# First attention scores of block 1 placed behind the first input products, a dearer instruction fetch in the list, and B22 staged in other buffers

## The chip, the cores and the metric

The kernel runs on one core of a Trainium2 chip. The core has five engines with an instruction queue each: TensorE (PE in the profile, its weight loads PEld), VectorE (DVE), ScalarE (ACT), GpSimd (POOL, idle here) and SyncE (SP, which only starts DMA transfers). An engine works through its queue in order; engines wait for each other by semaphores. The metric is the device time of one execution in microseconds (us), lower is better.

## The reference

Attention with a narrow window, then two feed-forward layers, on 2304 tokens of width 512:

```python
scores = q @ k.T / sqrt(64); heads 0-3: 0 <= rel < 32; heads 4-7: 0 <= rel < 128 and rel % 4 == 0
x = softmax(scores) @ v                    # 4 x 8 heads x 576 tokens x 64, laid out as (2304, 512)
h = x @ w_in;  P = a0 + a1 h + a2 h^2 + a3 h^3;  Q = 1 + |b0||h| + |b1| h^2
x = (P / (Q + 1e-6)) @ w_out               # layer 1, 512 -> 2048 -> 512
h = x @ w_in2; x = (max(h,0) + alpha min(h,0)) @ w_out2   # layer 2
```

## The kernel before

**Tiling.** Attention is cut into 18 units of 256 tokens and four heads each (a plain and a dilated one per token range). Layer 1 works on five token blocks (256, then four of 512 columns), with tokens along the free axis. For each block, 16 chunks ("items") of 128 hidden features are made by `inproj` (L608 to L619: products into one of two PSUM banks `ps_h`), go through the rational function on ScalarE and VectorE (`rat_1`, `rat_2`, the last step of the first block writing the tile `gl` at L650), and return through `outproj1` (L661, L669) into the four banks `ps_y`. Block 0 runs in plain fp32 (one product per weight tile, seen as two matmul records); the later blocks are split into a high and a low fp32r part with three products each. Layer 2 works on blocks of 384 tokens, two at a time, by a Strassen-like scheme: seven products `product` (L828) per pair of chunks, on operands named B11, T2, B21, T3, T4, T1 and B22 (`st_pair`, from L846).

**Attention of a unit.** `att_s` makes scores (a mask by bf16 matmuls, L468, then 32 fp32 products, L478) into two banks; `att_max`, `att_exp`, `att_den`, `att_norm`, `att_t` make the transposed probabilities `pts`; `att_pv` (L551) multiplies by the values; `att_hi`/`att_lo` copy the result into the layer's input `xh`, `xl`. Units 0 and 1 make block 0's input. Unit 2 is the first of block 1. Its scores stand in the loop at L984, ahead of block 0's input products.

**What sets the order.** The program is written as nested loops, and then `in_order_of_need` (L155) lists the instructions of each engine anew, up to 197 us of its own clock, by longest path to the end. It holds a cost per instruction (`_cost`, L111) and counts a delay on TensorE each time 256 instructions have been passed (`FETCH`, `FETCH_NS`, `FETCH_END`, L38 to L40 and L275). After that point the framework's scheduler orders the rest.

**The seam between the layers.** `x_load(0)` (L751) reads layer 1's output back from DRAM into staging tiles; B22's two halves were put into the attention buffers `p` and `pts` (L758). `x_combine` makes T1 to T4 from them, `x_place` splits each operand into its two parts (L726 on ScalarE, L727 on VectorE). The first pair's `v1` and `u2` (L863, L858) use the same two buffers `pts` and `p`.

**Weights.** The first weights arrive as 64-bit words and are converted on ScalarE (L392) and VectorE (L395, L397) before they can be multiplied.

Of the kernel before, what the change touches and what calls it, by code (L numbers as in the profile page):

```python
# [37 lines left out]
FETCH = 256  # L38
FETCH_NS = 3800
FETCH_END = 30e3  # L40
QB = 32
# [112 lines left out]

def in_order_of_need(tc, nc, places):  # L155

# [17 lines left out]
    for k, i in enumerate(todo):  # L174
# [36 lines left out]
        for kind, regions in (("r", reads), ("w", writes)):  # L211
            for place, p0, p1, f0, f1 in regions:
                have = seen.setdefault(place, [])
                if kind == "w":
                    have[:] = [x for x in have if not (p0 <= x[2] and x[3] <= p1 and f0 <= x[4] and x[5] <= f1)]
                have.append((k, kind, p0, p1, f0, f1))
    after = [[] for _ in range(n)]
    for k in range(n):
# [75 lines left out]
def attn_rational_prelu_kernel(  # L294
# [158 lines left out]
    def att_s(U, tags=("aS", "aP"), banks=None):  # L453
# [12 lines left out]
        for p in range(2):  # L466
            for j0, j1 in zip(runs[p], (*runs[p][1:], HALF)):
                nc.tensor.matmul(  # L468
                    out=s[p][:, j0 * CELL:j1 * CELL].rearrange("p (t k) -> p t k", k=CELL),
                    lhsT=ident16,  # L470
                    rhs=mask[kinds[p][j0]].unsqueeze(1).to_broadcast([128, j1 - j0, CELL]),
                    start=(j0 == 0), stop=False,
                )
        for jj in range(HALF):
            for i in range(HEADS):
                for p in range(2):
                    at = jj * HEADS + i
                    nc.tensor.matmul(  # L478
                        out=s[p][quad(i), jj * CELL:(jj + 1) * CELL],
                        lhsT=a["q"][rows(p), at * QB:(at + 1) * QB],  # L480
                        rhs=a["k"][rows(p), at * CELL:(at + 1) * CELL],
                        start=False, stop=(jj == HALF - 1),
                    )

    def att_max(U):
# [121 lines left out]
    def inproj(item):  # L607
# [9 lines left out]
        for k, (w, x) in enumerate(pairs):  # L617
            nc.tensor.matmul(out=hp, lhsT=w, rhs=x, start=(k == 0), stop=(k == len(pairs) - 1))  # L618
        h_t[item] = hp  # L619

    def pair_tiles(J):
# [84 lines left out]

    todo = []

    def out_some(k):
# [39 lines left out]
    def x_load(n):  # L749
# [3 lines left out]
        if n == 0:  # L753
# [3 lines left out]
            st["T3"], st["T1"] = t[:, :2 * BLK], t[:, 2 * BLK:]  # L757
            st["B22"] = [ap_.tile([128, BLK], F32, tag=s, name="st_b22") for s in ("p", "pts")]  # L758
            st["T2"] = st["T4"] = rawp.tile([128, 2 * DM], F32, tag="u", name="st_t2", bufs=1)[:, :2 * BLK]
# [224 lines left out]
    for k in range(4):  # L984
        if k < 3:
            att_s(k, sets[(k + 2) % 3])
        if k == 2:
            qk_load(3)
        if 0 <= k - 1 < 2:
            att_den(k - 1)  # L990
            att_norm2(k - 1)
        if k < 3:
            att_max(k)
            att_exp(k)
# [6 lines left out]
        with tc.high_priority(-100):  # L1001
            if k == 1:
                root_b1()
            for _ in range((0, 2, 2, 1)[k]):
                w_next(1)
    att_den(2)
    att_norm(2)
    att_t(2)

    for J in range(NP):  # L1010
        U = 2 + (J + 1) // 2
        new = J % 2 and U < NU
        last = J % 2 and U <= NU
        if last:
            banks = [bank(tag) for tag in ("aS", "aP")]
            att_pv(U - 1, banks)
            if new:
                v_load(U)
                att_s(U, banks=banks)
            if U + 1 < NU:  # L1020
                qk_load(U + 1)
        if new:
            att_max(U)
        if J >= NC and early and (J - NC) * 5 // 9 > (J - NC - 1) * 5 // 9:
            w_early(*early.pop(0))
        pair_tiles(J)
        for item in items[2 * J:2 * J + 2]:
            inproj(item)
        if J < NC // 2:
# [77 lines left out]
    out_some(len(todo))  # L1107
    in_order_of_need(tc, nc, slots)

# [76 lines left out]
```

## Time and profile before

| | |
|---|---|
| median of 3 runs | 875.23 us (874.51 to 875.78) |
| profiled execution | 874.21 us, of which the span of instructions is 872.4 us |
| TensorE busy | 845.8 us, 97% of the span |
| VectorE busy | 721.5 us, 83% |
| ScalarE busy | 559.9 us, 64% |
| mean granted TensorE clock | 0.938 of full speed |

The profile is one execution. The difference between 874.21 and 872.4 lies outside the first and last instruction. "Idle before" names what ended an engine's wait; "issue" means that nothing recorded ended it. The granted clock is given as a share of 2.4 GHz: 0.95 is the higher of its two levels, 0.50 the lower (1.2 GHz).

### The profile page before, as it was taken

How to read it: one execution, taken by the hardware profiler on the slowest of the kernel's cores; microseconds unless marked ns; L12 is line 12 of the kernel's file. 1: busy time of each engine (PE TensorE's matmuls, PEld its weight loads, DVE VectorE, ACT ScalarE, POOL GpSimd, SP SyncE). 2: the span in 40 equal slices, each digit the busy share in tenths (PEclk: the TensorE clock that was granted, in tenths of full speed). 3: DMA queues.
4: the chain of work that ended last, by engine and by line, in shares of the span. 5: the costliest groups of instructions: out<-in, count | busy, mean ns of one | idle time of the engine just before them, and what ended most of it. 6: DMA issues, size and time to landing. Idle time of an engine off the chain costs nothing. (4 is left out here: it accounts for less than half of the span.)

```text
span 872.4 us, 15592 instructions
## 1 busy us (share of the span) xinstructions
PE 845.8 (97%) x6258; PEld 719.1 (82%) x6260; DVE 721.5 (83%) x1066; ACT 559.9 (64%) x1092; POOL 0.2 (0%) x4
## 2 busy tenths in 40 slices
PE   7899999999999999999999899999999999999998
PEld 4677878888888777788888798998989989899896
DVE  4699999988989878899999698898976778767652
ACT  4799987777866786766766366557463546645424
POOL 0000000000000000000000000000000000000000
PEclk8799999999999999999999899999999999999999
DMA  9792211123631344322202233215220102300001
GB/s 351 308 371 97 64 61 49 53 100 122 236 121 56 117 160 173 116 83 94 87 25 97 85 142 100 97 61 154 82 86 24 49 25 79 119 28 25 0 1 73
DMA packets 33912, 90.93 MB, mean 104 GB/s; under 512 B 4016, under 2 KB 11568, under 8 KB 33840
## 3 DMA queue, kind: packets, MB, share of 16 engines
q1 hardware_dynamic: 33840, 89.94, 29.3%
q8 instruction: 49, 0.80, 0.4%
q14 instruction: 23, 0.19, 0.1%
HBM read 74.72 MB, written 15.20 MB: 103 GB/s over the span
## 5 line engine op out<-in xcount | busy, mean ns | idle before, releaser
L618 PE MATMUL ps_h<-xh,winh 128*128 128x512 f32 x256 | 102.1, 399 | 4.2 <-DVE tc L639 4.2
L618 PE MATMUL ps_h<-xl,winh 128*128 128x512 f32 x256 | 100.3, 392 | 0.6 <-DVE xl L588 0.6
L669 PE MATMUL ps_y<-gh,wouth 128*128 128x512 f32 x256 | 99.4, 390 | 0.9 <-ACT gh L658 0.9
L669 PE MATMUL ps_y<-gl,wouth 128*128 128x512 f32 x256 | 100.2, 391 | 0.0
L669 PE MATMUL ps_y<-gh,woutl 128*128 128x512 f32 x256 | 100.0, 391 | 0.0
L618 PE MATMUL ps_h<-xh,winl 128*128 128x512 f32 x256 | 99.8, 390 | 0.0
L636 ACT ACTIVATE ta<-ps_h,root 128x512 f32<-128x512 f32 (+1 forms) x80 | 52.4, 655 | 54.5 <-DVE tc L649 33.8
L689 PE MATMUL ps_y<-woutl,gh 128*128 128x512 f32 x192 | 74.9, 390 | 0.0
L689 PE MATMUL ps_y<-wouth,gl 128*128 128x512 f32 x192 | 74.9, 390 | 0.0
L689 PE MATMUL ps_y<-wouth,gh 128*128 128x512 f32 x192 | 74.8, 389 | 0.0
L726 ACT ACTIVATE st_a<-w 128x1024 fp32r<-128x1024 f32 x24 | 25.3, 1056 | 60.7 <-PE ps_h L828 55.2
L833 ACT ACTIVATE n<-h 128x768 f32<-128x768 f32 x48 | 40.5, 843 | 37.0 <-DVE gl L727 21.0
L618 PEld LDWEIGHTS ps_h<-xh,winh 128*128 128x128 f32 x256 | 48.0, 188 | 17.0 <-DVE tc L639 6.5
L637 ACT ACTIVATE tc<-ps_h,co 128x512 f32<-128x512 f32 (+1 forms) x80 | 59.8, 748 | 0.0
L835 DVE SCALAR_TENSOR_TENSOR n<-n,alp,h 128x768 f32<-128x768 f32 x48 | 48.7, 1016 | 13.0 <-ACT h L834 12.4
L638 DVE TENSOR_TENSOR tc<-tc,ps_h 128x512 f32<-128x512 f32 (+1 forms) x80 | 50.3, 628 | 10.0 <-ACT tc L637 9.8
L669 PEld LDWEIGHTS ps_y<-gh,wouth 128*128 128x128 f32 x256 | 48.1, 188 | 11.6 <-ACT gh L658 1.3
L618 PEld LDWEIGHTS ps_h<-xl,winh 128*128 128x128 f32 x256 | 48.1, 188 | 10.5 <-DVE xl L588 1.0
L669 PEld LDWEIGHTS ps_y<-gh,woutl 128*128 128x128 f32 x256 | 48.3, 189 | 10.0
L618 PEld LDWEIGHTS ps_h<-xh,winl 128*128 128x128 f32 x256 | 48.1, 188 | 10.2
L669 PEld LDWEIGHTS ps_y<-gl,wouth 128*128 128x128 f32 x256 | 48.2, 188 | 9.9
L639 DVE SCALAR_TENSOR_TENSOR tc<-tc,co,ps_h 128x512 f32<-128x512 f32 (+1 forms) x80 | 54.9, 686 | 0.2
(187 smaller groups left out, 2164.3 us busy)
## 6 DMA issues: line engine op xcount, KB each, us to landing
ld_qk<-in_qk_dram SPq DMA_DIRECT2D x16, 768.0 KB, 5.4
w<-w_dram_in SPq DMA_DIRECT2D x24, 512.0 KB, 3.2
raw<-in_w_in_dram SPq DMA_DIRECT2D x16, 512.0 KB, 5.3
raw_inh<-in_w_out_dram SPq DMA_DIRECT2D x13, 512.0 KB, 6.5
out_dram<-os SPq DMA_DIRECT2D x18, 256.0 KB, 2.1
raw_inh<-in_w_in_dram SPq DMA_DIRECT2D x8, 512.0 KB, 8.3
raw_outh<-in_w_in_dram SPq DMA_DIRECT2D x8, 512.0 KB, 9.1
raw_outh<-in_w_out_dram SPq DMA_DIRECT2D x8, 512.0 KB, 9.2
```

The source lines that it names most:

```text
L618: nc.tensor.matmul(out=hp, lhsT=w, rhs=x, start=(k == 0), stop=(k == len(pairs) - 1))
L636: nc.scalar.activation(out=ta, in_=hp, func=AF.Abs, scale=root)
L637: nc.scalar.activation(out=tc_, in_=hp, func=AF.Identity, scale=co[:, 3:4], bias=co[:, 2:3])
L638: nc.vector.tensor_tensor(out=tc_, in0=tc_, in1=hp, op=ALU.mult)
L639: nc.vector.scalar_tensor_tensor(out=tc_, in0=tc_, scalar=co[:, 1:2], in1=hp, op0=ALU.add, op1=ALU.mult)
L669: nc.tensor.matmul(out=yt, lhsT=w[:, m * 128:(m + 1) * 128], rhs=g, start=(c == 0 and i == 0), stop=(c == NC - 1 and i == len(pairs) - 1),)
L689: nc.tensor.matmul(out=yt, lhsT=g[:, tok], rhs=w, start=(first and i == 0), stop=(last and i == 2))
L726: nc.scalar.activation(out=hi, in_=t, func=AF.Copy)
L833: nc.scalar.activation(out=neg, in_=h, func=AF.Relu, scale=-1.0)
L835: nc.vector.scalar_tensor_tensor(out=neg, in0=neg, scalar=alp[:, c:c + 1], in1=h, op0=ALU.mult, op1=ALU.subtract, reverse1=True)
```

## The change

Five edits: (1) the list's fetch delay goes from 3800 to 6500 ns and is counted up to 45 instead of 30 us; (2) unit 2's scores, maximum, exponentials and normalisation move from the lead-in loop into the main loop's first pass (`J == 0`), behind the input products of block 0's items 0 and 1; (3) a list `late` ties the first score product of unit 2 behind the last input product of item 1; (4) the load of unit 3's q and k follows there; (5) B22's staging tiles take the buffers `v` (one) and `os` (one of two, otherwise used for output copies).

```diff
-FETCH_NS = 3800
-FETCH_END = 30e3
+FETCH_NS = 6500
+FETCH_END = 45e3
...
-def in_order_of_need(tc, nc, places):
+def in_order_of_need(tc, nc, places, late):
...
+    at = {i.name: k for k, i in enumerate(todo)}
+    for b, a in late:
+        behind[at[b]].add(at[a])
...
-            st["B22"] = [ap_.tile([128, BLK], F32, tag=s, name="st_b22") for s in ("p", "pts")]
+            st["B22"] = [
+                ldp.tile([128, BLK], F32, tag=s, name="st_b22", bufs=b) for s, b in (("v", 1), ("os", 2))
+            ]
...
-        if k < 3:
+        if k < 2:
             att_s(k, sets[(k + 2) % 3])
-        if k == 2:
-            qk_load(3)
...
-    att_den(2)
-    att_norm(2)
-    att_t(2)
...
-        new = J % 2 and U < NU
+        new = (J % 2 or J == 0) and U < NU
         last = J % 2 and U <= NU
-        if last:
+        if J == 0:
+            pair_tiles(J)
+            inproj(items[0])
+            ahead = inproj(items[1])
+        if new or last:
             banks = [bank(tag) for tag in ("aS", "aP")]
-            att_pv(U - 1, banks)
+            if last:
+                att_pv(U - 1, banks)
             if new:
-                v_load(U)
-                att_s(U, banks=banks)
+                if J:
+                    v_load(U)
+                scores = att_s(U, banks=banks)
+                if J == 0:
+                    late.append((scores, ahead))
```

The edits shift line numbers: L478, L551, L618, L669 of before are L482, L557, L624, L676 now; L636 to L659 are 7 higher, L726 and L727 are L734 and L735, L863 is L873.

**First place: TensorE, behind the attention values of units 0 and 1.** `ps_h_482` (before) and `ps_h_416` (now) are item 0, `ps_h_487` and `ps_h_421` item 1; `ps_aS`, `ps_aP` with `ld_qk_146` are unit 2's scores. Before:

```order
L551 MATMUL ps_y0_243<-p_288,ld_v_136 64x32 x2
L551 MATMUL ps_y1_244<-p_288,ld_v_136 64x32 x2
L618 MATMUL ps_h_482<-xh0_410,win0_308 128x256
L478 MATMUL ps_aS_320<-ld_qk_146 32x64
L478 MATMUL ps_aP_321<-ld_qk_146 32x64
```

Now:

```order
L557 MATMUL ps_y0_243<-p_288,ld_v_136 64x32 x2
L557 MATMUL ps_y1_244<-p_288,ld_v_136 64x32 x2
L624 MATMUL ps_h_416<-xh0_357,win0_308 128x256 x2
L624 MATMUL ps_h_416<-xh1_404,win0_308 128x256 x2
L624 MATMUL ps_h_421<-xh0_357,win0_308 128x256 x2
L624 MATMUL ps_h_421<-xh1_404,win0_308 128x256 x2
L482 MATMUL ps_aS_426<-ld_qk_146 32x64
L482 MATMUL ps_aP_427<-ld_qk_146 32x64
```

Seven of the eight products of items 0 and 1 moved ahead of unit 2's scores.

**Second place: TensorE, ahead of unit 2's values** (`ps_aS` from `pts` and `ld_v_148`). `ps_h_613` and `ps_h_618` are items 2 and 3, `ps_h_690` is item 4. Before:

```order
L618 MATMUL ps_h_613<-xh0_410,win2_314 128x256 x2
L618 MATMUL ps_h_613<-xh1_457,win2_314 128x256 x2
L618 MATMUL ps_h_618<-xh0_410,win2_314 128x256 x2
L618 MATMUL ps_h_618<-xh1_457,win2_314 128x256 x2
L551 MATMUL ps_aS_527<-pts_477,ld_v_148 64x32 x2
```

Now:

```order
L624 MATMUL ps_h_618<-xh0_357,win2_314 128x256 x2
L624 MATMUL ps_h_618<-xh1_404,win2_314 128x256 x2
L676 MATMUL ps_y0_735<-gl_506,wout0_360 128x256
L676 MATMUL ps_y1_736<-gl_506,wout0_360 128x256
L676 MATMUL ps_y2_737<-gl_506,wout0_360 128x256
L676 MATMUL ps_y3_738<-gl_506,wout0_360 128x256
L624 MATMUL ps_h_690<-xh0_357,win4_366 128x256 x2
L624 MATMUL ps_h_690<-xh1_404,win4_366 128x256
L557 MATMUL ps_aS_527<-pts_513,ld_v_148 64x32 x2
```

Four output products (they need `gl_506`, the first pair's result, and `wout0`) and three of item 4 moved ahead of unit 2's values.

**Third place: the seam, ScalarE.** `gh_5171` is the high part of layer 1's last pair, `v1_5189` the copy of the first Strassen product out of its bank `ps_h_5175`. Before:

```order
L726 ACTIVATE st_B22h_5161<-st_b22_4813 128x384
L646 ACTIVATE ta_5086<-tb_5087,c1t_109 128x1024
L726 ACTIVATE st_B22h_5161<-st_b22_4814 128x384
L647 ACTIVATE ta_5086<-ta_5086 128x1024
L658 ACTIVATE gh_5167<-tc_4998 128x1024
L658 ACTIVATE gh_5171<-tc_5088 128x1024
L863 ACTIVATE v1_5189<-ps_h_5175 128x384
```

Now:

```order
L734 ACTIVATE st_B22h_5161<-st_b22_4814 128x384
L653 ACTIVATE ta_5086<-tb_5087,c1t_109 128x1024
L654 ACTIVATE ta_5086<-ta_5086 128x1024
L873 ACTIVATE v1_5189<-ps_h_5175 128x384
L665 ACTIVATE gh_5171<-tc_5088 128x1024
```

`v1` now stands ahead of `gh_5171`, which needs VectorE's `tc_5088`.

The same place on VectorE: `gl_5168` and `gl_5172` are the low parts of layer 1's last two pairs, `st_s_5193`, `st_a_5199` and `st_s_5201` prepare the second Strassen pair. Before:

```order
L649 SCALAR_TENSOR_TENSOR tc_5088<-tc_5088,co_105,ta_5086 128x1024
L727 TENSOR_TENSOR st_B22l_5162<-st_b22_4813,st_B22h_5161 128x384
L650 SCALAR_TENSOR_TENSOR tc_5088<-tb_5087,tc_5088 128x1024
L727 TENSOR_TENSOR st_B22l_5162<-st_b22_4814,st_B22h_5161 128x384
L659 TENSOR_TENSOR gl_5168<-tc_4998,gh_5167 128x1024
L659 TENSOR_TENSOR gl_5172<-tc_5088,gh_5171 128x1024
L858 TENSOR_TENSOR u2_5190<-v1_5189,ps_h_5182 128x384
```

Now:

```order
L656 SCALAR_TENSOR_TENSOR tc_5088<-tc_5088,co_105,ta_5086 128x1024
L666 TENSOR_TENSOR gl_5168<-tc_4998,gh_5167 128x1024
L657 SCALAR_TENSOR_TENSOR tc_5088<-tb_5087,tc_5088 128x1024
L868 TENSOR_TENSOR u2_5190<-v1_5189,ps_h_5182 128x384
L749 TENSOR_TENSOR w32_5084<-w32_5084 128x256
L749 TENSOR_TENSOR st_s_5193<-w32_5084,st_s_5193 128x256
L666 TENSOR_TENSOR gl_5172<-tc_5088,gh_5171 128x1024
L735 TENSOR_TENSOR st_a_5199<-w32_5084,st_a_5198 128x1024
L735 TENSOR_TENSOR st_s_5201<-st_s_5193,st_s_5200 128x768
L421 TENSOR_TENSOR woutl2_5209<-w32_5206,wouth2_5208 128x1024
```

`gl_5168` and `u2` moved forward; the B22 splits stand a few rows earlier than before, and five operations that prepare later weights moved from ahead of this stretch to behind `u2`. On SyncE the load of B22's second half moved behind the four stores of layer 1's fourth block, and two weight loads of layer 2 moved behind eight loads of the next operands.

## Rows read from the trace of the kernel before

**Rows 1.** The page, part 1: busy time, share of the span, instructions by engine.

```profile
PE 845.8 (97%) x6258; PEld 719.1 (82%) x6260; DVE 721.5 (83%) x1066; ACT 559.9 (64%) x1092; POOL 0.2 (0%) x4
```

**Rows 2.** Busy time by stretch: length, engines with instruction counts, granted clock, DMA share.

```profile
20.00:30.00 10.00, 8.02 (x59) 6.27 (x46) 3.18 (x9) 4.21 (x21) 0.00 (x0) 0.56 1.03 408
...
50.00:80.00 30.00, 30.00 (x407) 25.26 (x407) 28.50 (x61) 29.79 (x84) 0.00 (x0) 0.95 0.67 248
80.00:120.00 40.00, 37.32 (x427) 30.61 (x426) 39.95 (x67) 37.10 (x77) 0.00 (x0) 0.95 0.20 63
120.00:200.00 80.00, 80.00 (x756) 65.93 (x755) 77.45 (x101) 60.11 (x155) 0.00 (x0) 0.95 0.18 59
...
490.00:860.00 370.00, 369.83 (x1852) 333.75 (x1851) 283.12 (x432) 196.69 (x255) 0.00 (x0) 0.95 0.19 66
```

**Rows 3.** Timeline of TensorE, 18 to 50 us: start, length, line, tiles, [idle before].

```profile
18.21 1.22 PE L618 MATMUL ps_h<-xh,win 128*128 128x256 f32 x2
...
22.46 0.31 PE L478 MATMUL ps_aS<-ld_qk 64*32 64x64 f32 x1 [1.98 <-issue]
...
22.83 7.95 PE L618 MATMUL ps_h<-xh,win 128*128 128x256 f32 x22
...
37.55 2.48 PE L618 MATMUL ps_h<-xh,win 128*128 128x256 f32 x8 [2.80 <-DVE tc L639]
...
43.53 3.77 PE L669 MATMUL ps_y<-gl,wout 128*128 128x256 f32 x16
49.28 1.16 PE L669 MATMUL ps_y<-gl,wout 128*128 128x256 f32 x4 [1.98 <-DVE gl L650]
```

**Rows 4.** DMA queues in the stretch 20 to 22 us: packets, MB, share.

```profile
q1 hardware_dynamic: 220, 0.79, 99.5%
q8 instruction: 1, 0.02, 3.3%
```

**Rows 5.** Busy time by granted clock in the lead-in, columns as in rows 2.

```profile
15.00:28.65 13.65, 10.75 (x149) 8.35 (x150) 6.12 (x12) 5.72 (x23) 0.00 (x0) 0.50 1.03 406
28.65:38.90 10.25, 7.05 (x100) 5.45 (x99) 7.97 (x17) 10.25 (x28) 0.00 (x0) 0.95 0.89 354
38.90:42.30 3.40, 3.40 (x71) 2.37 (x70) 2.26 (x5) 1.89 (x4) 0.00 (x0) 0.50 0.09 14
```

**Rows 6.** Timelines of ScalarE and VectorE, 25 to 40 us.

```profile
25.79 0.47 ACT L636 ACTIVATE ta<-ps_h,root 128x256 f32<-128x256 f32 x1 [6.40 <-PE ps_h L618]
...
26.76 0.42 DVE L638 TENSOR_TENSOR tc<-tc,ps_h 128x256 f32<-128x256 f32 x1 [2.37 <-ACT tc L637]
...
35.44 0.69 DVE L395 TENSOR_SCALAR wout<-wout 128x1024 uint32<-128x1024 uint32 x1
36.08 0.42 DVE L638 TENSOR_TENSOR tc<-tc,ps_h 128x256 f32<-128x256 f32 x1
...
38.74 0.68 DVE L650 SCALAR_TENSOR_TENSOR gl<-tb,tc 128x512 f32<-128x512 f32 x1
```

**Rows 7.** VectorE alone in one stretch: length, busy time (instructions), clock, DMA share, GB/s.

```profile
22.95:41.16 18.21, 11.44 (x25) 0.75 0.82 326
```

**Rows 8.** Timeline of TensorE at the seam.

```profile
485.01 0.45 PE L828 MATMUL ps_h<-st_B21h,st_a 128*128 128x384 f32 x1 [3.23 <-ACT v L863]
```

**Rows 9.** Timelines of ScalarE and VectorE at the seam.

```profile
483.52 1.06 ACT L658 ACTIVATE gh<-tc 128x1024 fp32r<-128x1024 f32 x1 [3.32 <-DVE tc L650]
484.48 0.47 ACT L863 ACTIVATE v<-ps_h 128x384 f32<-128x384 f32 x1
...
482.21 1.22 DVE L650 SCALAR_TENSOR_TENSOR tc<-tb,tc 128x1024 f32<-128x1024 f32 x1
483.35 0.55 DVE L727 TENSOR_TENSOR st_B22l<-st_b,st_B22h 128x384 fp32r<-128x384 f32 x1
483.81 2.35 DVE L659 TENSOR_TENSOR gl<-tc,gh 128x1024 fp32r<-128x1024 f32 x2
```

**Rows 10.** The stretch behind the stop at the seam, columns as in rows 2.

```profile
485.01:493.32 8.31, 8.31 (x32) 7.22 (x33) 4.87 (x9) 0.00 (x0) 0.00 (x0) 0.76 0.19 63
```

More of the change, by code (lines that the diff above doesn't have):

```diff
@@ L473, in att_s @@
                 )
+        products = []
         for jj in range(HALF):
@@ L477, in att_s @@
                     at = jj * HEADS + i
-                    nc.tensor.matmul(
+                    product = nc.tensor.matmul(
                         out=s[p][quad(i), jj * CELL:(jj + 1) * CELL],
@@ L483, in att_s @@
                     )
+                    products.append(product)
+        return products[0].ins.name
     def att_max(U):
@@ L617, in inproj @@
         for k, (w, x) in enumerate(pairs):
-            nc.tensor.matmul(out=hp, lhsT=w, rhs=x, start=(k == 0), stop=(k == len(pairs) - 1))
+            product = nc.tensor.matmul(out=hp, lhsT=w, rhs=x, start=(k == 0), stop=(k == len(pairs) - 1))
         h_t[item] = hp
+        return product.ins.name
     def pair_tiles(J):
@@ L707, in attn_rational_prelu_kernel @@
     todo = []
+    late = []
     def out_some(k):
@@ L991, in attn_rational_prelu_kernel @@
             att_norm2(k - 1)
-        if k < 3:
+        if k < 2:
             att_max(k)
@@ L1025, in attn_rational_prelu_kernel @@
             w_early(*early.pop(0))
-        pair_tiles(J)
-        for item in items[2 * J:2 * J + 2]:
-            inproj(item)
+        if J:
+            pair_tiles(J)
+            for item in items[2 * J:2 * J + 2]:
+                inproj(item)
         if J < NC // 2:
@@ L1107, in attn_rational_prelu_kernel @@
     out_some(len(todo))
-    in_order_of_need(tc, nc, slots)
+    in_order_of_need(tc, nc, slots, late)
 def _consts():
```

## The prediction

> **What bounds the kernel now.** I read the page's first part, then the busy time by stretch, then the timeline of TensorE where it is not full, and only there the other engines. The first part gives TensorE 845.8 us of a span of 872.4 [rows 1]; no rearrangement can take out more than the 26.6 us that are left, plus what a low clock costs inside the busy time. By stretch, TensorE is full from 50 to 80, from 120 to 200 and from 490 to 860 us; between 20 and 30 us it works 8.0 of 10 us, between 80 and 120 us 37.3 of 40 [rows 2]. VectorE works 39.95 of 40 us in that last stretch, so the kernel has a second engine without slack right behind the lead-in. What I look for, then, are TensorE's stops and its low clock, and whether VectorE can follow when one goes.
>
> The timeline of the lead-in shows four stops: 1.98 us before 22.46, with nothing recorded that ended it, 2.80 before 37.55 and 1.98 before 49.28, which VectorE ended [rows 3], and about 0.4 that is left of the 3.2 us idle between 28.65 and 38.90 when the 2.80 are taken off (10.25 less 7.05 busy) [rows 5]: 7.16 us in all. The granted clock was 0.50 from 15.00 to 28.65 and again from 38.90 to 42.30, just behind the 2.80 us stop [rows 5]. The seam has one more stop, 3.23 us before 485.01, which ScalarE's v ended [rows 8], and behind it 8.31 us at a mean clock of 0.76 [rows 10]. The change touches just these two places.
>
> **The lead-in.** TensorE reaches item 0 at 18.21 as before. Two matmul records of item 0 run there, then come the scores and the stop, and 22 more records at 22.83 [rows 3]. Now items 0 and 1 run first but for their last product, 16 records in all (a plain fp32 product leaves two, here called halves).
>
> *The stop before 22.46.* Nothing recorded ended it, and in its two microseconds the DMA engines were 99.5% busy with loads while one packet of the instruction queue passed [rows 4]. I read it as a wait for instructions, in the midst of 64-odd short score products, which use up instructions far faster than item products do. With 16 halves in their place, TensorE passes the same point of its queue about 24.6 us, some two microseconds after that packet was there. So the stop goes: 2.0 us. If it only moved with the scores, it would stay at 1.98.
>
> The Trainium skill ("Runtime: NRT & Kernel Launch", section "Instruction fetch mechanics") says that instructions come in blocks of 256 by the sequencer's own DMA queue and that crossing a block costs one DMA tail-bump, "mostly hidden". That speaks against the dearer delay in the list; the 1.98 us stop beside a full set of DMA engines disagrees with "hidden". By that rule the stop would have another cause and stay, and the sum would be 2.0 us smaller.
>
> *What TensorE loses otherwise.* At the high clock a half costs 3.77/16 = 0.236 us, while 22 of them from 22.83 on took 7.95, 0.36 each in a stretch that is mostly low [rows 3]. A half at the low clock I put at 0.42, so each low microsecond costs at most 1 - 0.236/0.42 = 0.44. From 18.21 to 28.65 and 38.90 to 42.30 there are 8.5 + 3.4 = 11.9 busy low microseconds, so at most 5.2 us; the short score and value products among them are less tied to the clock, and I take 4.7. Loss before: 7.2 + 4.7 = 11.9.
>
> After: in before the clock rose 5.8 us into the 22 products that nothing interrupts. Now an unbroken row begins at 18.21, and I take the rise at about 22.5: 4.3 low microseconds, 1.9 lost. Items 0 and 1 (16 x 0.236 = 3.8), the scores (1.4 by the same stretch of the timeline) and items 2 and 3 (3.8) then end at 18.21 + 1.9 + 9.0 = 29.1. TensorE's next instructions are output products, which need the first gl and half of wout0. Item 0's first step on ScalarE stood at 25.79, ahead of VectorE's 26.76 [rows 6]; with item 0 ready at 22.0 it stands 3.8 earlier, and VectorE's at 23.0. From there VectorE has seventeen operations up to the wout half: nine of about 0.7 (the conversions, and the 512-column steps like gl's 0.68), six of about 0.45, two of 0.17, together some 9.3 us, and in a row each begins some 0.05 to 0.08 before the record of the one ahead ends (35.44 + 0.69 against 36.08) [rows 6]: about 8.0, and 0.6 for two waits for ScalarE in the chain. That is 31.6. So there is a new stop, 2.5 us, where the 0.40 and the 2.80 were; I assume that the clock falls behind it for as long as it did in before, which cost 3.4 x 0.44 = 1.5. A second stop, ahead of item 7, is left of the 1.98 at 49.28: 1.7, by the same replay. Loss after: 1.9 + 2.5 + 1.5 + 1.7 = 7.6. TensorE's gain: 11.9 - 7.6 = 4.3.
>
> *Whether VectorE follows.* From 22.95 to 41.16 it works 11.44 of 18.21 us [rows 7], so 6.8 are idle. With item 0's result earlier by 3.8 the replay leaves about 3.1 idle for the same operations, a lead of 3.7. VectorE is full soon after, so I take the smaller: 3.7, between 1.3 (the fetch stop stays and the clock rises late, both from the sums above) and 5.7 (no new stop in the clock, half the first wait).
>
> *What the move delays.* Unit 2's scores come 5 us later, and with them maximum, exponentials and pts; its values are due ahead of item 4's end, some 36 us, and pts then stands behind six more VectorE operations, near 33. The load of unit 3's q and k follows those scores on SyncE; its own scores are due at about 39, some 13 us later. I cost both at nothing; without that cover each would cost its lateness, up to 2 us, inside the bounds.
>
> **The seam.** In before VectorE splits B22's second half at 483.35 (0.55 us) and first makes the last tc at 482.21 (1.22), ScalarE makes gh from it at 483.52 (1.06), and only then stands v at 484.48 [rows 9]. v needs neither: it stood in the queue behind gh, and it writes pts, which the staging of B22 held until the split had read it. Now B22 stages in other tiles, and v stands ahead of that gh; the third place of the change shows it. Its operand is a product that ended before TensorE's stop, so it comes before 481. But TensorE's next output products need gl too, which with its twin took 2.35 us from 483.81 [rows 9], so the first was there at about 485.0, no earlier than v. Taking only v away would buy nothing. gl_5168 is needed at 485.01 - 3.23 = 481.78 [rows 8], that is 3.2 us sooner. Ahead of it VectorE sheds the last tc (1.22) and, since five operations moved behind u2, three of 256 or 768 columns and two of 1024, at 1.22 for 1024 and 0.55 for 384, some 4.2: in all 5.4, against 3.2 wanted. The stop goes, 3.2 us, and gl comes at about 480.3.
>
> Behind the stop, 8.31 us ran at 0.76 instead of 0.95 [rows 10]; without it, 8.31 x (1 - 0.76/0.95) = 1.7. So 4.9 together; the bounds are 0 (TensorE waits for gl as long as it did for v) and 4.9. The five operations are then late by about 5 us, ready near 486, for a product that begins some 10 us later; the loads that stage B22 wait for the buffers v and os, which no attention or output needs there. Both at nothing.
>
> **The sum.** 3.7 + 4.9 = 8.6 us off the profiled execution of 874.2, so 865.6. The runs shown had 875.23 as median, 1.0 more; the forecast is **866.6 us**.
>
> **Rivals.**
> - *Only the seam.* The lead's gain is spent before 120 us, since VectorE works 39.95 of 40 us there [rows 2] and TensorE's stops there lengthen by what it won. For it: that row. Against it: VectorE itself is ahead by 3.7 in the replay. 875.2 - 4.9 = 870.3.
> - *Only the lead-in.* TensorE's stop at the seam becomes a wait for gl, as it was ready only at about 485.0 [rows 9]. Against it: 5.4 us of work removed from ahead of it. 875.2 - 3.7 = 871.5.
> - *More.* The new stop does not lower the clock (1.5 back) and TensorE's longer lead is kept in full (0.6), with a shorter wait for g (2.5 or part): about 862.5.
> - *Nothing.* The fetch stop moves with the scores, the new stops eat the rest, and at the seam gl is late: 874 to 876.
> - *Slower: the clock.* Two stops near the beginning (29 and 45 us) hold the granted clock at 0.50 from 32 us on. Each low microsecond costs 0.44 to 0.47 of work. The 1.5 already counted behind the first stop is part of it, so it eats the whole gain where it lasts (8.6 + 1.5)/0.47 = 21 us, past about 53 us; if it lasts until 60 us, 28 x 0.47 = 13.2, and 866.6 + 13.2 - 1.5 is about 878. For it: the fall from 0.95 to 0.50 behind the 2.80 us stop [rows 5]. Against: that one ended after 3.40 us, and TensorE is full, 30.00 of 30.00 us at 0.95, from 50 us [rows 2].
>
> The Trainium skill ("TensorE: Matmul & The Clock Gate", section "HAM oscillation — how this bites in real kernels") describes an array that waits for data between bursts, is throttled and starts cold each time; the slower rival is that rule here, and this trace bears it out only for single stops.
>
> **How the numbers follow.** Both gains 0.58 (863 to 869.5), only the seam 0.17, only the lead-in 0.08, more 0.05, nothing 0.05, slower 0.07. A measurement of this kernel can tell 0.2%, 1.75 us, from no change; so faster is 0.58 + 0.17 + 0.08 + 0.05 = 0.88, same 0.05, slower 0.07. The range from 862.5 to 871.5 takes in the first case, the seam alone, and half of the next two: just over 0.8. The likeliest case's own range is 863 to 869.5.
>
> **What would show it.** Right: no stop without a releaser in TensorE near 20 us, the first ta of item 0 near 22, one stop that VectorE ends at about 29 to 32, the last product of unit 3's values some 4 us earlier than before, no stop over 1 us at the seam, and a clock of 0.95 there. Wrong: a stop with no releaser that has moved to the next block of instructions, at the seam a stop that VectorE's gl ends, or a longer idle TensorE between 80 and 120 us than 2.7.

## The result, and the profile after

The changed kernel took 867.19 us as median of 4 runs (865.06 to 868.21), the kernel before 874.87 beside it: a ratio of 0.9911, 95% interval 0.9887 to 0.9934. In a later session, beside two other kernels, it took 867.00 (865.96 to 868.38) against 875.23, ratio 0.9899 (0.9882 to 0.9916). The forecast was 866.6 us. The profiled execution lasted 867.52 us, its span 865.7.

First the page's first part of the changed kernel, then its busy time by stretch (length, then PE, PEld, DVE, ACT, POOL with counts, granted clock, DMA share, GB/s).

```profile
PE 843.1 (97%) x6258; PEld 717.7 (83%) x6260; DVE 722.8 (83%) x1066; ACT 560.2 (65%) x1092; POOL 0.2 (0%) x4
```

```profile
20.00:30.00 10.00, 10.00 (x96) 7.54 (x94) 5.37 (x13) 6.55 (x15) 0.00 (x0) 0.79 1.03 410
50.00:80.00 30.00, 28.48 (x388) 24.34 (x378) 29.08 (x61) 30.00 (x90) 0.00 (x0) 1.00 0.64 247
80.00:120.00 40.00, 37.30 (x428) 30.29 (x427) 38.58 (x61) 37.14 (x83) 0.00 (x0) 1.00 0.22 69
120.00:200.00 80.00, 80.00 (x807) 65.81 (x809) 77.69 (x103) 59.50 (x144) 0.00 (x0) 1.00 0.17 56
490.00:860.00 370.00, 370.00 (x1849) 333.33 (x1848) 285.57 (x435) 198.90 (x258) 0.00 (x0) 1.00 0.20 66
```

Against [rows 1, 2]: TensorE is full between 20 and 30 us, where it worked 8.0 of 10; between 50 and 80 us it now stands 1.5 us, where it was full; the stretches from 80 us on are as full as they were.

The lead-in, TensorE's timeline (start, length, line, tiles, [idle before]), then ScalarE's and VectorE's, then the clock.

```profile
19.22 6.13 PE L624 MATMUL ps_h<-xh,win 128*128 128x256 f32 x16
...
26.06 3.98 PE L624 MATMUL ps_h<-xh,win 128*128 128x256 f32 x16
33.26 2.68 PE L676 MATMUL ps_y<-gl,wout 128*128 128x256 f32 x8 [3.21 <-DVE rd L522]
...
48.00 1.56 PE L624 MATMUL ps_h<-xh,win 128*128 128x256 f32 x6 [1.69 <-DVE tc L646]
...
55.75 0.48 PE L676 MATMUL ps_y<-gl,wout 128*128 128x256 f32 x1 [0.87 <-issue]
```

```profile
23.04 0.47 ACT L643 ACTIVATE ta<-ps_h,root 128x256 f32<-128x256 f32 x1 [2.60 <-PE ps_h L624]
...
24.00 0.42 DVE L645 TENSOR_TENSOR tc<-tc,ps_h 128x256 f32<-128x256 f32 x1 [3.64 <-ACT tc L644]
...
32.43 0.68 DVE L400 SCALAR_TENSOR_TENSOR wout<-raw_inh,wout 128x512 uint32<-128x512 uint32 x1
33.03 0.19 DVE L522 RECIPROCAL rd<-sm 128x8 f32<-128x8 f32 x1
```

```profile
17.29:24.12 6.83, 6.77 (x76) 5.75 (x77) 3.16 (x6) 2.49 (x7) 0.00 (x0) 0.50 1.03 408
24.12:34.36 10.24, 7.03 (x91) 5.34 (x90) 9.25 (x21) 9.33 (x33) 0.00 (x0) 1.00 1.02 409
34.36:37.77 3.41, 3.41 (x9) 2.72 (x9) 2.55 (x6) 3.41 (x10) 0.00 (x0) 0.50 0.66 261
```

Item 0 begins at 19.22 instead of 18.21 [rows 3]: unit 1's values stood 1.87 us (their row names ScalarE's conversion of win; VectorE's transpose of their p, 16.55 to 17.25, ended just before they began). Over all kernels below, with the same work up to there, it begins between 18.1 and 19.4 (21.4 in one that has extra work ahead), so times are taken from item 0's start from here on. Answering to [rows 3]: the 1.98 us stop without a releaser is gone, so are the 0.40 and the 2.80; there is one stop of 3.21, which ends with the conversion of half of wout0 (32.43 to 33.11; the row names its neighbour), one of 1.69, and one of 0.87 that nothing recorded ended. Answering to [rows 5]: 6.83 and 3.41 us at 0.50 instead of 13.65 and 3.40. Answering to [rows 6]: item 0's first step 2.75 us earlier on the clock of the trace, 3.8 from item 0's start.

The seam: TensorE, then ScalarE and VectorE.

```profile
480.17 0.34 PE L838 MATMUL ps_h<-st_B21h,st_a 128*128 128x384 f32 x1
480.35 0.34 PE L838 MATMUL ps_h<-st_B21l,st_a 128*128 128x384 f32 x1
480.52 0.44 PE L676 MATMUL ps_y<-gl,wouth 128*128 128x512 f32 x1
```

```profile
478.41 0.49 ACT L873 ACTIVATE v<-ps_h 128x384 f32<-128x384 f32 x1 [1.58 <-PE ps_h L838]
...
479.19 1.22 DVE L666 TENSOR_TENSOR gl<-tc,gh 128x1024 fp32r<-128x1024 f32 x1
480.33 1.22 DVE L657 SCALAR_TENSOR_TENSOR tc<-tb,tc 128x1024 f32<-128x1024 f32 x1
```

B21's first product follows without a stop, where 3.23 us stood [rows 8]. v comes at 478.41, gl ends at 480.41, a tenth of a microsecond before its first use (480.52); [rows 9] had them at 484.48 and behind 483.81. The clock stays at 1.00 there.

One place got worse that the change does not touch. TensorE, then the clock, then ScalarE and VectorE ahead of it:

```profile
314.44 0.80 PE L624 MATMUL ps_h<-xh,winh 128*128 128x512 f32 x1 [2.34 <-DVE tc L646]
315.03 0.63 PE L624 MATMUL ps_h<-xl,winh 128*128 128x512 f32 x1
...
317.87 0.39 PE L624 MATMUL ps_h<-xh,winl 128*128 128x512 f32 x1
```

```profile
314.25:317.67 3.42, 3.23 (x8) 2.56 (x9) 2.73 (x6) 3.42 (x8) 0.00 (x0) 0.50 0.06 25
```

```profile
304.72 0.66 ACT L395 ACTIVATE win<-raw 128x512 f32<-128x512 f32 x1 [0.46 <-DMA raw<-in_w_in_dram]
...
305.41 0.69 DVE L398 TENSOR_SCALAR win<-win 128x1024 uint32<-128x1024 uint32 x1 [1.24 <-ACT win L395]
306.02 0.41 DVE L496 TENSOR_REDUCE mx<-ps_aS 128x4 f32<-128x256 f32 x1
```

The same place in before, VectorE and TensorE:

```profile
307.13 0.41 DVE L490 TENSOR_REDUCE mx<-ps_aS 128x4 f32<-128x256 f32 x1
...
321.43 0.69 DVE L395 TENSOR_SCALAR win<-win 128x1024 uint32<-128x1024 uint32 x1
...
315.54 0.50 PE L618 MATMUL ps_h<-xh,winh 128*128 128x512 f32 x1 [0.46 <-DVE tc L639]
```

A conversion of a later weight (win6) now stands ahead of the maximum of unit 15 on VectorE (the expectations below call it unit 13), waits 1.24 us for ScalarE, and that for its load. In before it stood 16 operations further back, behind that maximum. TensorE then stops 2.34 us for a bank, where before had 0.46, and runs at half clock for 3.4.

The account, in us earlier (-) than before, each from item 0's start in its own trace (before: item 0 at 18.21, the points at 205.62, 275.48, 343.39, 478.11, 503.91 and 868.33; the changed kernel: 19.22, then 203.39, 273.29, 342.99, 477.14, 497.49, 861.62). The first point lies in a stretch in which TensorE is full in all of them:

| kernel | the 353rd input record | the 1009th value record | the 617th input record | layer 2's first product | layer 1's last output product | last product |
|---|---|---|---|---|---|---|
| changed | -3.2 | -3.2 | -1.4 | -2.0 | -7.4 | -7.7 |
| changed, again | -4.1 | -4.1 | -2.5 | -3.1 | -8.5 | -7.5 |
| B22 alone | +2.5 | +2.7 | +2.3 | +1.7 | -3.5 | -2.9 |
| half of B22 | +0.1 | +0.1 | -0.3 | -0.4 | +0.5 | +0.8 |
| lead-in alone | -3.8 | -3.8 | -1.7 | -2.3 | -5.4 | -4.8 |
| fetch constants alone | -5.0 | -4.3 | -5.7 | -5.1 | -5.2 | -4.8 |
| old constants in the changed | -3.9 | -4.0 | -4.4 | -4.8 | -9.8 | -9.6 |
| list to 205 us in the changed | -4.9 | -3.3 | -3.5 | -4.1 | -9.3 | -8.5 |
| constants and B22, scores not moved | -4.7 | -3.6 | -3.4 | -4.7 | -10.0 | -9.7 |
| the same, list to 220 us | -5.5 | -4.2 | -5.0 | -5.6 | -10.7 | -10.2 |

So in the first profile the lead-in won 3.2, the middle took 1.2 back (3.4 at the stop, the rest regained later), the seam won 5.5. Each row is one execution, and some lie well off their kernel's median: B22 alone 2.0 us above it, the lead-in alone 1.5 above, the list to 205 us 0.9 below, the constants alone 0.7 below. The two rows with B22 have before's order up to the seam and still show +2.5 and +0.1, so a difference of 1 to 2 us between two rows shows little; the steps along one row are steadier.

### The profile page after: what moved, and what is told of

Read it like the earlier page. It is cut to its first block, busy times and chain, and to the rows that moved or that the text cites. A ratio compares the mean times of both kernels' runs of the same rounds, so it can differ in the third digit from the quotient of the medians.

```text
span 865.7 us, 15595 instructions
## 1 busy us (share of the span) xinstructions
PE 843.1 (97%) x6258; PEld 717.7 (83%) x6260; DVE 722.8 (83%) x1066; ACT 560.2 (65%) x1092; POOL 0.2 (0%) x4
## 4 chain that ended last, share of the span: by engine, by line
PE 74%; DVE 11%; ACT 11%; issue 2%; DMA 1%; SPq 0%; ACTq 0%
PE ps_h L838 20%; PE ps_y L696 15%; PE ps_h L624 14%; PE ps_y L676 13%; PE ps_aS L696 4%; PE ps_aP L696 4%; ACT p L513 3%; ACT p L528 2%; DVE tc L656 2%; DVE tb L652 1%; DVE tc L646 1%; ACT ta L643 1%; DVE tc L657 1%; DVE tc L645 1%; ACT tc L644 1%
## 5 line engine op out<-in xcount | busy, mean ns | idle before, releaser
L624 PE MATMUL ps_h<-xh,winh 128*128 128x512 f32 x256 | 102.8, 401 | 3.9 <-DVE tc L646 3.8
L624 PE MATMUL ps_h<-xl,winh 128*128 128x512 f32 x256 | 100.6, 393 | 1.1 <-DVE xl L594 1.1
L624 PE MATMUL ps_h<-xh,winl 128*128 128x512 f32 x256 | 100.3, 392 | 0.0
L676 PE MATMUL ps_y<-gh,wouth 128*128 128x512 f32 x256 | 99.2, 390 | 0.6 <-ACT gh L665 0.6
L676 PE MATMUL ps_y<-gl,wouth 128*128 128x512 f32 x256 | 99.7, 389 | 0.0
L676 PE MATMUL ps_y<-gh,woutl 128*128 128x512 f32 x256 | 99.7, 389 | 0.0
L624 PEld LDWEIGHTS ps_h<-xh,winh 128*128 128x128 f32 x256 | 48.4, 189 | 17.2 <-DVE tc L646 6.1
L645 DVE TENSOR_TENSOR tc<-tc,ps_h 128x512 f32<-128x512 f32 (+1 forms) x80 | 50.1, 627 | 12.8 <-ACT tc L644 12.7
L845 DVE SCALAR_TENSOR_TENSOR n<-n,alp,h 128x768 f32<-128x768 f32 x48 | 48.8, 1016 | 13.7 <-ACT h L844 13.0
L624 PEld LDWEIGHTS ps_h<-xl,winh 128*128 128x128 f32 x256 | 48.5, 190 | 11.3 <-DVE xl L594 1.8
L676 PEld LDWEIGHTS ps_y<-gh,wouth 128*128 128x128 f32 x256 | 48.1, 188 | 10.8 <-ACT gh L665 1.0
L624 PEld LDWEIGHTS ps_h<-xh,winl 128*128 128x128 f32 x256 | 48.4, 189 | 10.3
L734 ACT ACTIVATE st_a<-w 128x1024 fp32r<-128x1024 f32 x24 | 25.4, 1057 | 48.3 <-PE ps_h L838 45.2
L653 ACT ACTIVATE ta<-tb,c1t 128x1024 f32<-128x1024 f32 (+1 forms) x40 | 43.2, 1080 | 20.5 <-DVE tb L652 20.4
L676 PEld LDWEIGHTS ps_y<-gh,woutl 128*128 128x128 f32 x256 | 48.0, 188 | 9.9
L676 PEld LDWEIGHTS ps_y<-gl,wouth 128*128 128x128 f32 x256 | 48.0, 188 | 9.9
```

The lines of the kernel that those rows point to most:

```text
L624: product = nc.tensor.matmul(out=hp, lhsT=w, rhs=x, start=(k == 0), stop=(k == len(pairs) - 1))
L645: nc.vector.tensor_tensor(out=tc_, in0=tc_, in1=hp, op=ALU.mult)
L653: nc.scalar.activation(out=ta, in_=tb, func=AF.Ln, bias=c1t)
L676: nc.tensor.matmul(out=yt, lhsT=w[:, m * 128:(m + 1) * 128], rhs=g, start=(c == 0 and i == 0), stop=(c == NC - 1 and i == len(pairs) - 1),)
L734: nc.scalar.activation(out=hi, in_=t, func=AF.Copy)
L845: nc.vector.scalar_tensor_tensor(out=neg, in0=neg, scalar=alp[:, c:c + 1], in1=h, op0=ALU.mult, op1=ALU.subtract, reverse1=True)
```

## The experiments

One part was answered by the instruction order alone: without the `late` tie the changed kernel's program is the same on PE, DVE and ACT, row for row. With the costs as they stand, the tie does nothing.

**B22 alone**

```diff
-            st["B22"] = [ap_.tile(..., name="st_b22") for s in ("p", "pts")]
+            st["B22"] = [ldp.tile(..., name="st_b22", bufs=b) for s, b in (("v", 1), ("os", 2))]
```

> Before with B22's two staging tiles in v and os, and nothing else of the change; every engine's order up to the seam is word for word that of before, behind it that of the changed kernel. Theory (the seam alone is worth the 3.23 us stop and the low clock behind it): no stop over 0.5 us at the seam, 5.0 to 5.5 us off, ratio 0.9940 (869.6 us). Rival (the seam's gain in the changed kernel came from VectorE's lead out of the lead-in): the stop becomes a wait for gl and stays over 2 us, ratio above 0.998.

870.38 us (869.13 to 872.36) against 874.60, ratio 0.9948 (0.9930 to 0.9967). No stop at the seam. Its profiled execution was its slowest run, with a lead-in 2.7 us worse than before's by the same order: 6.8 us at half clock behind the stop of 2.85, and 3.4 more later, where [rows 5] has 3.40 once. From layer 2's first product to layer 1's last, 5.2 us are won in it (+1.7 to -3.5); the timed runs show 4.2, less than the 5.0 to 5.5 expected. Behind the seam the order is not quite that of the changed kernel: three of B21's products, not two, stand ahead of the first that needs gl. The theory holds; the part needs no lead out of the lead-in.

**Half of B22**

```diff
+            st["B22"] = [ldp.tile(..., tag="v", bufs=1), ap_.tile(..., tag="pts")]
```

> Before with only the first half of B22 staged elsewhere (in v), the second still in pts. Every engine's order is that of before, word for word. Theory (v waits for the split of what lies in pts, and the scheduler lets gl and u2 go first only when that wait is gone): the seam's stop of about 3.2 us ahead of v and the low clock behind it stay, ratio 1.000 within 0.002. Rival (any relief of the staging buffers starts the loads and splits of B22 earlier): the stop falls by 1 us or more, 1 to 3 us off.

874.89 us (872.64 to 878.16) against 875.24, ratio 1.0003 (0.9986 to 1.0020). TensorE at the seam:

```profile
484.83 0.69 PE L831 MATMUL ps_h<-st_B21h,st_a 128*128 128x384 f32 x1 [3.33 <-ACT v L866]
```

The stop is all there. Freeing `p` alone does nothing, so what held v, and with it the scheduler's place for gl and u2, needs the half in `pts` to go; whether that half alone is enough was not run.

**The lead-in alone** (the changed kernel, B22 in `p` and `pts` again)

> The changed kernel with B22 staged in p and pts again: lead-in alone. Theory (lead-in wins 3.2 us, of which a new stop near 312 us takes 2.6 back): the same stop of about 2.3 us near 312 us, the seam's stop of about 3.2 us ahead of v still there, 2 to 2.6 us off in all, ratio 0.997 to 0.9978. Rival (the stop near 312 us belongs to the other staging): no stop over 1 us near 312 us, 3.2 to 3.7 us off, ratio 0.996.

868.85 us (868.12 to 870.33) against 874.60, ratio 0.9938 (0.9920 to 0.9955): over twice what I expected. The stop in the middle is there (2.60 us, at 314.08), so it belongs to the lead-in's edits. But the seam's stop is not the old one. TensorE, then ScalarE:

```profile
481.37 0.45 PE L836 MATMUL ps_h<-st_B21h,st_a 128*128 128x384 f32 x1 [1.38 <-ACT v L871]
481.65 0.34 PE L836 MATMUL ps_h<-st_B21l,st_a 128*128 128x384 f32 x1
...
483.06 0.51 PE L676 MATMUL ps_y<-gl,wouth 128*128 128x512 f32 x1 [0.35 <-DVE gl L666]
```

```profile
480.82 0.49 ACT L871 ACTIVATE v<-ps_h 128x384 f32<-128x384 f32 x1 [3.20 <-DVE st_B22l L735]
481.90 1.06 ACT L665 ACTIVATE gh<-tc 128x1024 fp32r<-128x1024 f32 x1 [0.58 <-DVE tc L657]
```

1.7 us instead of 3.2, and no low clock behind it. Here the scheduler has put v ahead of the last gh although `pts` is still borrowed, and v stands 3.20 us for the split of B22's second half: the wait that the prediction inferred, seen by itself. B21's other products now stand ahead of the first that needs gl. So the two parts are not independent: 4.2 and 5.8 alone make 10.0, together 7.7 to 8.2; on top of the lead-in B22 is worth 1.9 to 2.5.

**The fetch constants alone**

```diff
-FETCH_NS = 3800
-FETCH_END = 30e3
+FETCH_NS = 6500
+FETCH_END = 45e3
```

> Before with the two fetch constants of the changed kernel (6500 ns, up to 45 us) and nothing else. Unit 2's scores stay behind the first product of item 0; unit 3's scores move ahead of item 4 and the first output products behind item 5. Theory (the lead-in's gain is the place of unit 2's scores, not the constants): the stop without releaser of about 2 us stays in those scores, item 0's first step on ScalarE stays near 25 to 26 us, time within 1.5 us of before, ratio 0.998 to 1.002. Rival (the constants carry the gain): the stop shrinks below 0.5 us, 3 us or more off, ratio 0.9965 or less.

871.09 us (870.35 to 872.23) against 875.24, ratio 0.9957 (0.9942 to 0.9972). My theory falls. The stop without a releaser is still there (1.79 us), item 0's first step is late (26.54), the seam's stop is there in full (3.35 us), and still 4.2 us are won. The stop in the middle is there as well (2.24 us, at 312.34), without moved scores.

**Constants and B22 without moved scores**

> Before with the fetch constants and the staging of B22 of the changed kernel, but unit 2's scores left where they were (no moved loop, no tie). Theory (the fetch constants alone reorder the lead-in well enough, as they won about 4 us alone; moving the scores adds nothing to the time): within 1.5 us of the changed kernel run beside it, ratio to before 0.989 to 0.993, with the stop without releaser still near 21 to 23 us. Rival (the changed kernel's lead-in needs the moved scores, and the constants' gain alone came from the seam's wait being shorter there): 3 us or more slower than the changed kernel, ratio 0.995 or more.

865.62 us (865.23 to 865.81), the changed kernel beside it 867.00 (865.96 to 868.38), before 875.23: ratio 0.9884 (0.9866 to 0.9901). The ranges do not overlap; it is the faster of the two. TensorE, then the clock:

```profile
23.43 0.31 PE L478 MATMUL ps_aS<-ld_qk 64*32 64x64 f32 x1 [1.98 <-issue]
...
32.11 1.99 PE L618 MATMUL ps_h<-xh,win 128*128 128x256 f32 x8 [0.92 <-DVE tc L639]
...
38.20 3.72 PE L618 MATMUL ps_h<-xh,win 128*128 128x256 f32 x16 [1.80 <-DVE tc L639]
```

```profile
17.20:27.44 10.24, 8.14 (x139) 6.33 (x140) 7.16 (x14) 4.55 (x10) 0.00 (x0) 0.50 1.03 409
27.44:60.00 32.56, 29.04 (x393) 24.35 (x392) 28.73 (x63) 32.56 (x113) 0.00 (x0) 1.00 0.98 373
```

Here the instruction stop stays in unit 2's scores, and the lead-in is as good: VectorE's stops are 0.92 and 1.80, and none near 49 us, where [rows 3] has 2.80 and 1.98, and the clock stays at its high level behind 27.44, up to a stop of 2.21 us at 313.05. I put that down to unit 3's scores ahead of item 4, which the dearer fetch brings; no run has them alone. On top of the constants alone, B22 is worth 5.5 us here (871.09 to 865.62).

**The old constants in the changed kernel**, twice

> The changed kernel with the fetch delay at 3800 ns up to 30 us again. Unit 2's scores stay behind item 1; unit 2's values now stand ahead of the first output products, and with them half of VectorE's order from 23 us on. Theory (the lead-in's gain is the place of the scores; the dearer fetch only sets what comes behind): no stop without releaser near 20 us, the lead-in's gain within 1.5 us of the changed kernel's, ratio to before 0.990 to 0.993. Rival (the dearer fetch is what gives the gain): 2 us or more slower than the changed kernel, ratio 0.994 to 0.996.

> The changed kernel with the old fetch constants again, beside the changed kernel. Theory (it avoids the stop near 312 us, worth about 3 us with its low clock, and has a lead-in some 0.6 us worse and a seam alike): 1.5 to 2.5 us faster than the changed kernel, ratio to before 0.988 to 0.9905. Rival (their difference was chance between sessions): within 0.8 us of it.

865.32 us (864.74 to 866.21), ratio 0.9895 (0.9875 to 0.9915); then, beside the changed kernel, 865.64 (864.60 to 866.94), ratio 0.9885 (0.9868 to 0.9902), 1.4 us under the changed kernel's 867.00, with ranges that overlap. The scores behind item 1 alone give the lead-in as well, and no stop over 0.5 us near 312. Its lead-in has a stop elsewhere for which the row names nothing. TensorE, then VectorE:

```profile
32.01 0.30 PE L557 MATMUL ps_aS<-pts,ld_v 32*64 32x32 f32 x4 [2.60 <-issue]
```

```profile
31.19 0.71 DVE L541 STREAM_TRANSPOSE pts<-p 128x512 f32<-128x512 f32 x1 [2.15 <-ACT p L528]
```

It is no wait for instructions: it ends 0.1 us behind VectorE's transpose that makes unit 2's pts, its operand (31.90), and by the count of instructions the place where before had stopped was passed at 24.1 us without a wait. It ends 12.7 us behind item 0's start, where the changed kernel's 3.21 us wait for VectorE ends 14.0 us behind it.

**The changed kernel again**

> The changed kernel again, beside the kernel without the moved scores and the one with the old fetch constants, on one chip. Theory: 867 us, ratio 0.991, the same stops as in its first profile (about 3.2 us near 30 us, 1.7 near 46 us, 2.3 near 312 us). Rival (the stop near 312 us is chance): no stop over 1 us there, and 865 us or less.

867.00 us. The same stops came (3.21, 1.70 and 2.16, the last at 312.65): the one in the middle is no chance.

**Does the stop follow the instruction count?** Tiny products, 8 columns each, behind the last warm-up product; 24 in before, 58 in the changed kernel.

```diff
+    extra = [nc.tensor.matmul(out=idle[:, :8], lhsT=warm[:, :128], rhs=warm[:, :8], ...) for _ in range(24)]
```

> Before with 24 tiny matmuls (8 columns, with their weight loads 48 instructions) behind the last warm-up product, all orders else as in before. Theory (the 1.98 us stop is TensorE waiting for its next 256 instructions, which land when they land): the stop begins 48 instructions earlier in the score products, that is near the first of unit 2's 32 pairs instead of the 28th, and ends at about the same time, so it is 2.5 to 3.2 us long. Rival (the stop belongs to the data or banks of those scores): it stays at the same product with about 2.0 us.

> The changed kernel with 58 such tiny matmuls (116 instructions) at the same place, all orders else as in the changed kernel. The boundary of 256 instructions that it passes in unit 2's scores near 25.7 us then falls at item 0's first product, near 20 us. Theory (items 0 and 1 ahead of the scores only win because TensorE comes to the boundary after the instructions have landed): a stop without releaser of 2 to 4 us comes back just at item 0, and item 0's first step on ScalarE is that much later. Rival (the stop went because the scores moved): no stop over 0.5 us without a releaser between 17 and 28 us.

TensorE of the first, then of the second:

```profile
22.77 0.31 PE L488 MATMUL ps_aS<-ld_qk 64*32 64x64 f32 x1 [2.33 <-issue]
```

```profile
21.41 6.15 PE L634 MATMUL ps_h<-xh,win 128*128 128x256 f32 x16 [2.71 <-issue]
```

In before 56 of unit 2's 64 score records stand ahead of the stop, with 24 more products 32 do: it moved by exactly 24. I had set the length at 2.5 to 3.2 and the place near the first pair; it is 2.33 and the 17th pair: 24 products are 12 pairs, and they pass in less than half a microsecond. In the second kernel the stop that the changed kernel had lost is back, just ahead of item 0, whose first step on ScalarE came at 25.23. Each ran once, 881.93 and 871.39 us; the first has another stop without a releaser, 2.36 us before 56.02, so these times say nothing on the first stop's worth.

**The stop in the middle**: the list, which ends at 197 us of its own clock, ends at 205 in the changed kernel, and at 220 in the kernel with constants and B22.

```diff
-ORDERED = 197e3
+ORDERED = 205e3
```

> The changed kernel with the written-out list reaching to 205 instead of 197 us of its own clock. This leaves the lead-in and the seam as they are and puts the conversion of win6 (loaded about 300 us) behind unit 13's maximum on VectorE again, where before had it. Theory (the 2.34 us stop near 312 us and the low clock behind it come from VectorE standing 1.24 us at that conversion for a load): the stop falls under 1 us and 2.5 to 3.5 us more are won, 864 us, ratio to before 0.9875. Rival (the lead is used up there by VectorE's amount of work, whatever its order): the stop moves to another item between 280 and 370 us, the time stays at 867 us, ratio 0.991.

> Before with the fetch constants and the staging of B22, unit 2's scores not moved, and the written-out list reaching to 220 instead of 197 us of its own clock; the conversion of win6 then stands behind unit 13's maximum on VectorE again. Theory (the stop of 2.2 us near 312 us and the 3.4 us of low clock behind it come from that conversion waiting for its load, and go): the stop under 1 us, 1.5 to 3 us off the 865.6 us of the same kernel without it, ratio to before 0.985 to 0.987. Rival (what goes there comes back as VectorE's stops between 230 and 370 us): 865 to 866 us, ratio 0.9885.

866.61 us (865.66 to 867.33), ratio 0.9907 (0.9888 to 0.9925); and 865.69 (865.17 to 866.45), ratio 0.9895 (0.9874 to 0.9916). In both the conversion is behind the maximum again and the stop near 312 us falls to 0.47 and 0.40, as the theory has it (with the list to 205 us the order at the seam changes by one product too). In both the time stays, as the rival has it: the kernels without this edit have ratios of 0.9911 and 0.9899 (the changed kernel, twice), and of 0.9884. What TensorE waited for most between 200 and 370 us (sum, times, longest), the changed kernel, then with the list to 205:

```profile
PE ps_h L624 <- DVE tc L646: 3.8, 3, 2.3
```

```profile
PE ps_h L624 <- DVE tc L646: 4.9, 6, 1.2
```

Three stops became six with a larger sum. The profiles still show 0.5 to 1 us less in the end; the timed runs do not resolve it.

## Why the prediction was right, and where its reasons were not

**The fetch stop: the mechanism is shown, its weight is not.** It is a wait for instructions; it follows the count, it ends 1.3 to 1.5 us behind the packet (in before the packet ends at 21.16 and TensorE resumes at 22.46, in the second kernel with tiny products 19.94 and 21.41), and it goes when TensorE comes later. In the changed kernel the packet of instructions went by at 21.2 to 22.3 us, and TensorE passed that point, by the count of instructions, near 25.7. So the Trainium skill's "mostly hidden" ("Runtime: NRT & Kernel Launch", section "Instruction fetch mechanics") holds in the changed kernel, and does not where TensorE comes early: there it stopped 1.8 to 2.7 us. The DMA engines are as full of loads in the one case as in the other (share 1.03 from 20 to 30 us). But the step that counted it as 2.0 us of gain failed as a reason: with B22 staged alike, the kernel that keeps it in full (constants alone, 865.6 us) is as fast as the one that loses it (moved scores alone, 865.3 and 865.6), and faster than the changed one. And a sign that the prediction had named for being wrong came in small: a stop without a releaser 768 instruction records further on (0.87 us at 55.75, 1.15 in the second profile), a whole number of the blocks of 256 that the list counts.

**The lead-in's sum: right.** Foreseen were VectorE's first operation at 23.0 and half of wout0 at 31.6, measured 24.00 and 33.11 with item 0 1.0 late, so right and 0.5 late; a new stop of 2.5 and a second of 1.7, measured 3.21 and 1.69; the clock up at 22.5, measured 24.12, so 23.1 (the 5.8 us that before took would have given 24.0; the 22.5 was chosen); and low for 3.4 us behind the stop, measured 3.41. Foreseen gain 3.7, measured 3.2 and 4.1 in two profiles at 200 us. One sign came short: unit 3's last value product is 1.9 and 2.2 us earlier in them, from item 0's start, not some 4. (The 16 records ahead of the scores are all eight products of items 0 and 1; the prediction's "but for their last product" does not go with its 16.) What failed is the claim behind it, that the moved scores make it: the constants alone and the moved scores alone each do, and together they are no better. They do it in different ways. The constants alone keep the instruction stop (1.79 us) and shorten VectorE's, to 0.92 and 1.80 where [rows 3] has 2.80 and 1.98. The moved scores alone lose the instruction stop and keep waits for VectorE (0.96, 2.60, 0.61 and 2.19). Either way less of the first 60 us runs at the low clock, 10.2 to 13.7 us against 17.1; but profiles with before's own order have 13.7 to 20.5, so how much of the gain that is stays open.

**The middle: a term left out.** I priced what moves in the lead-in and at the seam, and nothing behind 200 us. There the framework orders what the list does not, from a state that the lead-in has changed, and the four rows of the account with both lead-in edits lose 0.8 to 1.5 us of their lead between the 353rd input record and layer 2's first product, where the two rows with before's order gain 0.5 and 0.8. It is a piece of the first rival (VectorE takes the lead back), 200 us later than I had placed it. That the place of win6's conversion makes the stop near 312 us is shown, and so is what brings that place: every kernel here with the dearer constants and the list to 197 us has it, moved scores or not, and none with the old constants. But the stop does not decide what the middle costs: the constants alone and the constants with B22 have it (2.24 and 2.21 us) and have lost nothing by layer 2's first product, and the list to 205 us removes it and loses 0.8 all the same. What takes the lead there stays open.

**The seam: right, a little more in the profiles.** 4.9 foreseen, 5.2 to 5.5 in the profiles of the changed kernel and of B22 alone, 4.2 in the timed runs of B22 alone. v stood waiting for the split of what lies in `pts` (its row in the lead-in alone; half of B22 agrees), and gl came earlier along with it. It was foreseen at 480.3, 1.5 us ahead of its use; it came at 480.41, but TensorE was there 1.3 us sooner, and 0.1 us of margin was left (with the old constants in the changed kernel, TensorE stands 0.25 us for it). Whether v's relief without an earlier gl would buy nothing was not tried: in each kernel that frees `pts` the scheduler moves both. The parts don't add up because the order at the seam also hangs on the lead-in: with the constants alone it is before's, with a stop of 3.3 us, and with the lead-in alone v and B21's products have already moved, with 1.7 left to win. Why the scheduler does so these runs do not show.

**The sum.** 3.7 + 4.9 = 8.6 foreseen; 7.7 and 8.2 measured: the middle's 1.2 off, some 0.5 more at the seam. That the number came within 0.6 us is in part luck: the loss in the middle was in no term, the gain in front did not hang on the edit that was priced, and one order's lead-in differs by 2.5 us between profiles. Nothing spoke for the slower rival; a third stop of 2.3 us with low clock came, but single, and TensorE was busy behind it.

## What to carry to other kernels

Two edits that each give the lead-in's gain need not give it twice: undo each one in the finished kernel before keeping it. Here constants and staging alone take 865.6 us, 1.4 less than with the moved loop. When a buffer is borrowed, look for what waits for its release: giving B22 other staging tiles moved v, gl and u2. And a gain at the front has to pass every stretch in which a second engine is full; a stop removed there may come back as several small ones, and the largest stop in sight need not be what costs the time.

## What the runs showed of the hardware

The granted clock of 0.95 in before's profile and 1.00 in the others makes no difference to the products of 512 columns. Between 120 and 200 us, before, then the changed kernel:

```profile
L669 PE MATMUL ps_y<-gl,wouth 128*128 128x512 f32 x54 | 21.0, 389 | 0.0
```

```profile
L676 PE MATMUL ps_y<-gl,wouth 128*128 128x512 f32 x56 | 21.8, 389 | 0.0
```

389 ns both. Block 0's plain fp32 halves of 256 columns do differ. Sixteen of them without a wait, in before, in the changed kernel, and in half of B22, which has before's order at 1.00:

```profile
62.66 3.76 PE L669 MATMUL ps_y<-gl,wout 128*128 128x256 f32 x16
```

```profile
60.38 3.62 PE L676 MATMUL ps_y<-gl,wout 128*128 128x256 f32 x16
```

```profile
63.01 3.62 PE L669 MATMUL ps_y<-gl,wout 128*128 128x256 f32 x16
```

Block 0 has sixteen times as many as one row, so by an estimate from these rows up to 2.2 us of before's profile, the base of the account, are this. The total does not resolve it: a later run of before had a span of 872.4 us at a mean of 0.990, where the profile had 872.4 at 0.938. The fall to 0.50 costs more: 0.63 instead of 0.39 us for a product of 512 columns at 315 us. And the same order can meet the low clock differently: the kernels with constants and B22 have a stop of 1.80 us with no low clock behind it, and one of 1.83 with 3.4 us of it. What decides that these runs don't show.
